# An mLSTM with a bilinear expert layer: a written order for the first two chunks, two more chunks in bfloat16 parts, and weight conversion in written slots beside the first block

## The chip, the core and the metric

The kernel runs on one core of a Trainium2 chip. Its engines are TensorE (PE in the profile; PEld is its weight load), VectorE (DVE), ScalarE (ACT), GpSimd (POOL) and SyncE (SP), which here issues the transfers. The metric is the device time of one execution in microseconds. A change is called faster or slower when it moves the time by more than 2%.

## What is computed

Four sequences of 768 steps with eight heads of 40 columns go through an mLSTM with an exponential input gate and a running maximum; the result, 3072 tokens of 320 columns, goes through a bilinear layer of 1536 columns. The expert weights are float64 in memory, everything else is float32.

```python
for t in range(S):
    m_new = np.maximum(f_gate[:, :, t] + m, i_gate[:, :, t])
    f_stab = np.exp(f_gate[:, :, t] + m - m_new)
    i_stab = np.exp(i_gate[:, :, t] - m_new)
    C = f_stab[..., None, None] * C + i_stab[..., None, None] * np.einsum('bhd,bhe->bhde', vt, kt)
    n = f_stab[..., None] * n + i_stab[..., None] * kt
    h_tilde = np.einsum('bhde,bhe->bhd', C, qt)
    denom = np.maximum(np.abs(nq), 1.0)              # nq = n . q
    y[:, :, t] = sigmoid(o_gate[:, :, t]) * h_tilde / denom
x = y.transpose(0, 2, 1, 3).reshape(B * S, H * D)    # 3072 x 320
out = ((x @ w_a) * (x @ w_b)) @ w_out                # 320 x 1536, 320 x 1536, 1536 x 320
```

## The kernel before

**Chunks.** The time axis is cut into six chunks of 128 steps; with four sequences that makes 24 chunks, numbered n, sequence by sequence within a time chunk. Chunks 0 to 3 are the first time chunk and have no state to read. For each chunk the kernel forms a decay matrix E, the scores q k^T (tile pS), their product with E, the product with the values (pV), the contribution of the carried state (pI, from the second time chunk on), the state's update (pU), the division by the denominator and the output gate (osig), and a transpose (pX) into xh and xl, the two halves that the expert layer reads.

**Two ways for a chunk.** Chunks below NF32 = 6 are computed in float32 (begin_a, begin_b, begin_i, begin_c: float32 transposes pT on TensorE, then float32 matmuls). The others are split into three bfloat16 parts (stage_a, stage_v, stage_b, stage_i, stage_c: the parts are laid out in the tiles qks and turned by DMA transposes into T; products are sums of bfloat16 matmuls). The tiles qks serve two purposes: until the weights are converted they are scratch (step) of the conversion, so stage_a finishes the conversion first. Chunks below NE = 4 get E by one-hot matmuls from stk, which holds the gate sums in three bfloat16 parts (begin_e, tile pE); the others read it from memory (g_dram).

**Blocks.** The expert layer runs in nine blocks of 2, 2, 3, 3, 3, 3, 3, 2 and 3 chunks (moe_block). Each has 12 column groups ff. Per ff there are 16 up matmuls into two PSUM tiles pu (line 693), a copy g (line 699), the product g (line 700), its rounding gh (line 702) and the rest gl (line 704), and two groups later three down matmuls per chunk into pd (line 664). The weights and gh, gl are in the rounded float32 kind.

**Weights.** 32 stages (weight_stages) hold the pieces of w_a, w_b and w_out. A stage is loaded as raw 64-bit words, and turned on the chip into a rounded high part and a low part: ACT reads sign and exponent (line 334), DVE makes the words (lines 335, 336, 338), ACT rounds (line 350), TensorE forms the difference in a PSUM tile pc (lines 352, 353), and DVE adds (line 354). The tiles pu and pc share the pool ps_up of three buffers. For the stages whose rows come from two matrices (last), the parts are put in place by four transfers w<-ct on SP (lines 358, 359).

**What sets the order.** The program is written as generators. The start (function start, 50 steps of priority ahead) is interleaved with the conversion every second piece; afterwards block 0 and 1 are interleaved with pieces of the attention of the following chunks and one piece of conversion in six. The order on each engine is then made by a scheduler that runs a model of the engines and takes what its model has ready, by priority; BEHIND makes the weight loads wait for the issue of certain chunk loads. Each engine executes its own list strictly in order.

The whole gate table is made first (gates): a scan of 768 columns gives the running maximum, and the tables for all chunks follow before the first chunks are multiplied.

## Time and profile before

| | |
|---|---|
| time, median of 3 runs (lowest to highest) | 575.65 us (572.2 to 579.28) |
| the profiled execution, from the first to the last instruction | 572.6 us |
| instructions | 12609 |
| TensorE busy | 547.5 us (96%) |
| VectorE busy | 396.8 us (69%) |
| ScalarE busy | 265.9 us (46%) |
| GpSimd busy | 129.1 us (23%) |
| moved by DMA | 68.34 MB, mean 119 GB/s |
| mean granted TensorE clock | 0.973 |

The page gives the profiled execution's span and no other time for it; the median lies 3.05 us above that span. The busy time of an engine counts the time in which at least one of its instructions runs. A digit of the slices is the busy share of one fortieth of the span, 14.3 us, in tenths. PEclk is the share of the full clock that TensorE was granted. A timeline row has the start and the duration in us, the engine, the line of the kernel, the operation and what it writes and reads; square brackets hold the engine's idle time before it and what ended that. A group row has the busy time in us and the mean duration in ns behind the first bar, and the idle time ahead of the group behind the second. A row of the chain of waits has start and length in us and how many instructions were merged.

### The profile page before, as it was taken

Reading aid. Unit: us, or ns where it says so; the run is one execution under the profiler, and the core shown is the slowest. Engines: PE = TensorE matmul, PEld = TensorE weight load, DVE = VectorE, ACT = ScalarE, POOL = GpSimd, SP = SyncE. Lnnn points to the kernel's source line nnn. Section 1 sums busy time; section 2 is a strip of 40 time slices with the busy share of each in tenths; the row PEclk is TensorE's granted clock in tenths of the full one; section 3 lists DMA queues with packets and bytes.
Section 4 is the critical chain, followed back from the end, with each engine's and each line's share of the span. In section 5 each row is a group of like instructions: output and inputs, shape, how many; then the busy total and the mean of one; then the engine's idle time right before and its main releaser. Section 6 shows DMA issues by size and latency. Waiting matters only on the chain.

```text
span 572.6 us, 12609 instructions
## 1 busy us (share of the span) xinstructions
PE 547.5 (96%) x4864; PEld 526.0 (92%) x4864; DVE 396.8 (69%) x884; ACT 265.9 (46%) x634; POOL 129.1 (23%) x182
## 2 busy tenths in 40 slices
PE   3799999999999999999999999999999999999997
PEld 2688999889999989999999999999999899999996
DVE  6866788975578777499649976698648654954342
ACT  3644565673255465255825554555525921411111
POOL 3021331463213222123303330332111200200000
PEclk9857999989999999999999999999999999999999
DMA  9979945365244966267954676478538603200000
GB/s 206 285 184 278 228 111 107 73 153 121 63 103 115 190 118 142 75 123 148 155 109 110 150 150 131 115 159 159 109 97 129 154 2 99 59 2 23 1 2 34
DMA packets 199863, 68.34 MB, mean 119 GB/s; under 512 B 184476, under 2 KB 193084, under 8 KB 199804
## 3 DMA queue, kind: packets, MB, share of 16 engines
q1 hardware_dynamic: 199804, 67.55, 54.6%
q8 instruction: 38, 0.62, 0.5%
q14 instruction: 21, 0.17, 0.1%
HBM read 41.11 MB, written 5.97 MB: 82 GB/s over the span
## 4 chain that ended last, share of the span: by engine, by line
PE 85%; DVE 4%; ACT 4%; DMA 3%; issue 1%; SPq 1%; POOL 1%; ACTq 0%; DVEq 0%; POOLq 0%
PE pu L693 45%; PE pd L664 21%; PE pV L503 4%; PE pU L527 3%; PE pS L451 3%; PE pV L807 2%; PE pS L764 2%; PE pX L600 2%; PE pI L477 1%; PE pc L352 1%; DMA qk<-in_k_dram 1%; PE pT L751 1%; ACT gbc L396 1%; DMA T<-qks 1%; DMA gbc<-g_dram 1%
## 5 line engine op out<-in xcount | busy, mean ns | idle before, releaser
L693 PE MATMUL pu<-xh,w 128*128 128x384 f32 (+1 forms) x1080 | 278.1, 325 | 2.8 <-ACT g L699 1.9
L693 PE MATMUL pu<-xl,w 128*128 128x384 f32 (+1 forms) x648 | 208.4, 323 | 0.0
L693 PEld LDWEIGHTS pu<-xh,w 128*128 128x128 f32 x1080 | 192.0, 190 | 5.3 <-ACT g L699 2.9
L664 PE MATMUL pd<-w,gh 128*128 128x320 f32 x576 | 127.2, 311 | 0.0
L700 DVE TENSOR_TENSOR g<-pu,g 128x384 f32<-128x384 f32 (+1 forms) x108 | 54.9, 508 | 100.3 <-ACT g L699 51.6
L693 PEld LDWEIGHTS pu<-xl,w 128*128 128x128 f32 x648 | 123.2, 190 | 0.1
L664 PEld LDWEIGHTS pd<-w,gh 128*128 128x128 f32 x576 | 97.2, 189 | 0.3
L664 PE MATMUL pd<-w,gl 128*128 128x320 f32 x288 | 85.8, 312 | 0.0
L699 ACT COPY g<-pu 128x384 f32<-128x384 f32 (+1 forms) x90 | 39.6, 440 | 95.1 <-PE pu L693 88.3
L396 ACT ACTIVATE gbc<-gbc,gtab 128x128 f32<-128x128 f32 x160 | 49.1, 389 | 16.3 <-POOL gbc L389 16.2
L664 PEld LDWEIGHTS pd<-w,gl 128*128 128x128 f32 x288 | 53.1, 189 | 0.1
L704 DVE TENSOR_TENSOR gl<-g,gh 128x384 fp32r<-128x384 f32 (+1 forms) x92 | 50.6, 550 | 2.1
L493 POOL TENSOR_TENSOR vw<-va,gtab 128x336 f32<-128x336 f32 x14 | 10.8, 769 | 161.7 <-PE pU L527 139.0
L702 DVE CAST gh<-g 128x384 fp32r<-128x384 f32 (+1 forms) x108 | 41.2, 382 | 2.4
L389 POOL TENSOR_SCALAR_AFFINE_SELECT gbc<-gbc 128x1024 f32<-128x1024 f32 x20 | 23.9, 1197 | 61.6 <-DMA va<-in_v_dram 33.2
L579 POOL TENSOR_TENSOR osig<-osig,den 128x320 f32<-128x320 f32 x24 | 19.6, 816 | 65.0 <-DVE den L574 45.8
L418 DVE TENSOR_TENSOR r<-qk,qks 128x320 f32<-128x320 f32 x36 | 18.0, 502 | 19.8 <-ACT qks L414 17.0
L414 ACT CAST qks<-qk 128x320 bf16<-128x320 f32 x36 | 16.3, 452 | 31.2 <-DMA T<-qks 27.7
L673 ACT COPY o<-pd 128x320 f32<-128x320 f32 x24 | 8.8, 434 | 42.9 <-PE pd L664 42.9
L424 ACT COPY qks<-qks 128x640 bf16<-128x640 bf16 x36 | 26.0, 726 | 0.4
L460 DVE TENSOR_TENSOR gbc<-gbc,pb 128x512 f32<-128x512 f32 x36 | 24.5, 704 | 2.3 <-ACT pb L458 2.0
L456 DVE TENSOR_TENSOR gbc<-pS,gbc 128x512 f32<-128x512 f32 x36 | 23.6, 679 | 3.3 <-PE pS L451 3.3
(133 smaller groups left out, 878.9 us busy)
## 6 DMA issues: line engine op xcount, KB each, us to landing
gbc<-g_dram SPq DMA_DIRECT2D x20, 512.0 KB
va<-in_v_dram SPq DMA_DIRECT2D x24, 160.0 KB
qk<-in_q_dram SPq DMA_DIRECT2D x24, 160.0 KB
qk<-in_k_dram SPq DMA_DIRECT2D x24, 160.0 KB
osig<-in_o_gate_dram SPq DMA_DIRECT2D x24, 160.0 KB
raw<-in_moe_w_out_dram SPq DMA_DIRECT2D x12, 320.0 KB
out_dram<-o SPq DMA_DIRECT2D x24, 160.0 KB
raw<-in_moe_w_a_dram SPq DMA_DIRECT2D x8, 384.0 KB
```

Source lines behind the costliest of these rows:

```text
L389: nc.gpsimd.affine_select(E, E, pattern=[[0, H], [1, P]], compare_op=ALU.is_ge, fill=-1e30, base=0, channel_multiplier=-1,)
L396: nc.scalar.activation(E[:, h], E[:, h], AF.Exp, bias=beta[:, h:h + 1])
L424: nc.scalar.copy(qks[:, 0, :, lo:lo + 2 * D], qks[:, 1, :, D - lo:3 * D - lo])
L456: nc.vector.tensor_tensor(E, pS, E, op=ALU.mult)
L460: nc.vector.tensor_tensor(E, E, pb[:, 0], op=ALU.subtract)
L503: nc.tensor.matmul(pv[:, h], pb[i][:, h % HH, :], vb[j][:, h], start=(x == 0), stop=(x == len(terms) - 1),)
L664: nc.tensor.matmul(pd[t][:, 0:DM], a[:, cols], w, start=(ff == 0 and first), stop=(ff == NF - 1 and last),)
L693: nc.tensor.matmul(acc[j], a, r, start=(x == 0), stop=(x == len(terms) - 1),)
L699: (nc.vector.tensor_copy if ff in [1, 2] else nc.scalar.copy)(g, acc[0])
L700: nc.vector.tensor_tensor(g, acc[1], g, op=ALU.mult)
L702: nc.vector.tensor_copy(gh, g)
L704: (nc.gpsimd if kb * 12 + ff < 16 else nc.vector).tensor_tensor(gl, g, gh.bitcast(F32), op=ALU.subtract)
```

## The change

- The first two chunks are emitted in one written order (start), and in_order ties each instruction to the one before it on its engine, so that the scheduler cannot move it. The gates of the first time chunk are computed alone (gates_first); the rest of the table (gates_rest) is cut into pieces that are placed beside block 0. The gate loads go out first, one on SP and one on ACT's queue. Filler matmuls on zeros (busy, and dense for chunks 2 and 3) are added on TensorE.
- NF32 goes from 6 to 4: chunks 4 and 5 are computed in bfloat16 parts, as the later ones.
- The weight stages are listed in the order in which block 0 uses them: a down piece of a group ahead of the up pieces of the next. The conversion is split in four steps, signs, words, leading and rests. Stages 0 to 4 are converted in the start, stages 5 to 31 in a written loop in which each stage has a slot beside seven or eight matmuls of block 0. The loop also places the pieces of gates_rest and, from stage 8 on, one piece of the attention of chunks 2 and 3 per stage.
- The stages with rows of two matrices are put in place by copies on ACT and additions on DVE, 64 rows each, instead of transfers.
- In block 0 gh is made by ACT instead of DVE. load_g is issued later within a chunk (at U), and the product with the output gate is done by DVE for chunks 0 and 1.

```diff
-    NF32 = 6
+    NF32 = 4
...
+    def dense(n, bank, count):
+        if NS <= n < NF32:
+            for _ in range(count):
+                nc.tensor.matmul(bank[:, 0:H * DV], zero[:, 0:P], zero, start=True, stop=True)
...
-        nc.vector.tensor_tensor_scan(m, f, i, -1e30, op0=ALU.add, op1=ALU.max)
+        nc.vector.tensor_tensor_scan(m, f[:, 0:P], i[:, 0:P], -1e30, op0=ALU.add, op1=ALU.max)
...
+        yield from ups(0)
+        for g in range(NG):
+            yield from down(3 * g)
+            if g + 1 < NG:
+                yield from ups(g + 1)
+            yield from down(3 * g + 1)
+            yield from down(3 * g + 2)
...
+        with in_order():
+            rest = start()
...
+    with in_order():
+        for x in range(5, len(stages) + 3):
+            if x < len(stages):
+                words(x)
+                if x + 1 < len(stages):
+                    signs(x + 1)
+                leading(x)
+            for _ in range(4 if x >= 12 else 3):
+                next(lead)
+            if 5 <= x - 2 < len(stages):
+                rests(x - 2)
+            for _ in range(4):
+                next(lead)
+            if x < 14 or x % 3 == 0:
+                next(rest, None)
+            if x >= 8:
+                next(att)
...
-            nc.vector.tensor_copy(gh, g)
+            (nc.vector.tensor_copy if kb > 0 else nc.scalar.copy)(gh, g)
```

The written start, with the generators that it drives, in the order of the text (run(x, k) takes k pieces of x, busy(k) issues k fillers, fetch(k) loads the stages up to k):

```python
busy(13); f, i = gates_load()
load_qk(0); load_qk(1); load_v(0); load_v(1); fetch(2); load_o(0, (0, 1)); fetch(5); load_o(0, (2, 3)); fetch(9)
m0, w = gates_first(f, i); rest = gates_rest(f, i, m0)
run(a0, 1); busy(2); run(a0); busy(2); run(b0, 1); busy(2); run(e0); run(rest, 2); run(begin_a(1)); signs(0)
run(b0); words(0); run(e1); gates_w(w); signs(1); leading(0); run(b1); gate_o(0, slice(0, 2)); rests(0); words(1)
run(begin_c(0)); weigh(0); run(begin_c(1)); leading(1); run(stage_f(0)); signs(2); states.append(stage_u(0))
run(states[0], 1); load(NS); fetch(11); weigh(1); run(stage_f(1)); rests(1); words(2); leading(2)
busy(4); run(d0); busy(4); rests(2); signs(3); words(3); leading(3); states.append(stage_u(1)); run(states[1], 1)
load(NS + 1); fetch(len(stages)); busy(4); run(d1); busy(4); signs(4); rests(3); busy(8); words(4)
gate_o(0, slice(2, B)); rests(4)
```

Three places show how rows move. The first is VectorE's list where the gates begin, at the start of the program; g_f and g_i (after: g_xh, g_xl) are the gate inputs, g_m (after: g_first) the working tile, cx_1_103 holds stk. Before:

```order
L194 SCALAR_TENSOR_TENSOR g_m<-g_f,g_i 32x768
L195 MEMSET g_f 32x1
L196 TENSOR_TENSOR g_f<-g_f,g_m 32x127
L201 TENSOR_TENSOR g_m<-g_i,g_m 32x128
L197 TENSOR_TENSOR g_f<-g_f,g_m 32x127
L198 SCALAR_TENSOR_TENSOR g_m<-one,g_f 32x128
L202 TENSOR_TENSOR g_m<-g_m 32x128
L207 TENSOR_SCALAR g_tab<-g_m 32x128
L211 COPY cx_1_103<-g_m 32x256
L213 TENSOR_TENSOR g_m<-g_m 32x256
L335 TENSOR_SCALAR cw<-qks_90 128x384
L211 COPY cx_1_103<-g_m 32x256
```

After, the same place on VectorE:

```order
L231 SCALAR_TENSOR_TENSOR g_first<-g_xh,g_xl 32x128
L232 TENSOR_TENSOR g_xh<-g_xh,g_first 32x127
L233 MEMSET g_xh 32x1
L234 TENSOR_TENSOR g_xh<-g_xh,g_first 32x127
L235 TENSOR_TENSOR g_first<-g_xl,g_first 32x128
L236 SCALAR_TENSOR_TENSOR g_first<-one,g_xh 32x128
L239 TENSOR_TENSOR g_first<-g_first 32x128
L242 COPY cx_1_103<-g_first 32x256
L245 TENSOR_TENSOR g_first<-g_first 32x256
L242 COPY cx_1_103<-g_first 32x256
L245 TENSOR_TENSOR g_first<-g_first 32x256
L242 COPY cx_1_103<-g_first 32x256
```

The scan over 768 columns has become one over 128, and the conversion (cw) has gone from between the rows that fill stk. The scan of the other 640 columns stands behind the last of these rows.

The second place is VectorE's list in the middle of block 0, at its column group ff = 4; cw, qks and cr belong to the conversion of a stage, w to its last step, g, gh to the block, gbc to a chunk's E. Before:

```order
L700 TENSOR_TENSOR g_4_931<-pu_4_1_908,g_4_931 128x256
L335 TENSOR_SCALAR cw<-qks_91 128x384
L354 TENSOR_TENSOR w_934<-pc_936,cw 128x320
L702 CAST gh_4_960<-g_4_931 128x256
L354 TENSOR_TENSOR w_978<-pc_980,cw 128x384
L336 TENSOR_SCALAR qks_91<-cw 128x384
L338 SCALAR_TENSOR_TENSOR cr<-raw_869,qks_91 128x384
L335 TENSOR_SCALAR cw<-qks_90 128x384
L770 TENSOR_TENSOR gbc_611<-pS_1_1160,gbc_611 128x4x128
```

After, at the same column group:

```order
L410 TENSOR_SCALAR cw<-qks_91 128x384
L411 TENSOR_SCALAR qks_91<-cw 128x384
L413 SCALAR_TENSOR_TENSOR cr<-raw_467,qks_91 128x384
L790 TENSOR_TENSOR g_4_899<-pu_4_1_870,g_4_899 128x256
L442 TENSOR_TENSOR w_864<-pc_940,cw 128x384
L863 TENSOR_TENSOR gbc_636<-pS_0_910,gbc_636 128x4x128
L863 TENSOR_TENSOR gbc_636<-pS_1_911,gbc_636 128x4x128
L410 TENSOR_SCALAR cw<-qks_90 128x384
L411 TENSOR_SCALAR qks_90<-cw 128x384
L413 SCALAR_TENSOR_TENSOR cr<-raw_469,qks_90 128x384
```

The three rows of a stage now stand together, one finishing row (w) of an earlier stage follows each three, gh has left the list, and the E of this place belongs to chunk 2 (before: chunk 4).

The third place is TensorE's list where block 1 ends; pu with 128x256 and pd belong to block 1, pu with 128x384 to block 2, pS to the scores of a chunk, pU to a state. Before:

```order
L664 MATMUL pd_0_1515<-w_1385,gh_9_2226 128x320 x2
L664 MATMUL pd_0_1515<-w_1385,gl_9_2228 128x320
L664 MATMUL pd_1_1516<-w_1385,gh_9_2226 128x320 x2
L664 MATMUL pd_1_1516<-w_1385,gl_9_2228 128x320
L693 MATMUL pu_0_0_2319<-xh_1686,w_366 128x384
L693 MATMUL pu_0_0_2319<-xl_1687,w_366 128x384
```

After, at the end of block 1:

```order
L612 MATMUL pU_2261<-vw_2205,qk_84 64x42 x8
L754 MATMUL pd_0_1540<-w_1370,gh_11_2514 128x320 x2
L754 MATMUL pd_1_1541<-w_1370,gh_11_2514 128x320 x2
L754 MATMUL pd_0_1540<-w_1370,gl_11_2516 128x320
L754 MATMUL pd_1_1541<-w_1370,gl_11_2516 128x320
L529 LDWEIGHTS T_1_2194
L529 MATMUL pS_0_2302<-T_0_2177,T_1_2194 128x128
```

Before, block 2 begins while block 1's last two column groups are still to be summed. After, block 1 ends completely, and the scores, the state product and the value product of chunk 7 and the transpose of chunk 6 stand ahead of the first up matmul of block 2.

More of the change, by code (lines that the diff above doesn't have):

```diff
@@ L1 @@
-from contextlib import ExitStack
+from contextlib import ExitStack, contextmanager, nullcontext
 import concourse.bass as bass
@@ new lines, in leading, with rests @@
+    def leading(x):
+        if not turn(2, x):
+            return
+        n, W, r = held[x]
+        w = ws[x] = rpool.tile([P, 2, n], F32R, tag=f"s{x}", name=f"w{x}")
+        h = w[:, 0]
+        if len(stages[x]) > 1:
+            h = cpool.tile([P, WCH], F32R, tag="ct", name="ct", bufs=2)
+        nc.scalar.copy(h, W)
+        held[x] += [w, h]
+    def rests(x):
+        leading(x)
+        if not turn(3, x):
+            return
+        ready[0] = x + 1
+        n, W, r, w, h = held.pop(x)
+        pc = ps_up.tile([P, NTB], F32, tag="pu", name=f"pc{x}")[:, :n]
+        nc.tensor.matmul(pc, eye[0], r, start=True, stop=False)
+        nc.tensor.matmul(pc, eye[1], h, start=False, stop=True)
+        if len(stages[x]) > 1:
+            for j in range(2):
+                rows, other = (slice(64 * i, 64 * i + 64) for i in (j, 1 - j))
+                nc.scalar.copy(w[rows, j], W[rows])
+                nc.vector.tensor_tensor(w[other, j], pc[rows], W[rows], op=ALU.add)
+        else:
+            nc.vector.tensor_tensor(w[:, 1], pc, W, op=ALU.add)
@@ L361, in weights @@
[L361 to L368 removed]
+                words(x)
                 yield x
             if x > 0:
[L371 removed]
+                rests(x - 1)
                 yield x
@@ L831, in room, with busy, run @@
             return spool.tile([P, H * P], F32, tag="x", name=name)
+        states = []
         def start():
-            g = gates()
-            next(g)
+            warm = ps_dn.tile([P, 512], F32, tag="pd1", name="warm")
+            def busy(count):
+                for _ in range(count):
+                    nc.tensor.matmul(
+                        warm[:, 0:H * DV], zero[:, 0:P], zero, start=True, stop=True
+                    )
+            def run(x, count=99):
+                for _ in range(count):
+                    if next(x, "end") == "end":
+                        return
+            busy(13)
+            f, i = gates_load()
@@ new lines, in start @@
+            run(a0, 1)
+            busy(2)
+            run(a0)
+            busy(2)
+            run(b0, 1)
+            busy(2)
+            run(e0)
+            run(rest, 2)
+            run(begin_a(1))
+            signs(0)
+            run(b0)
+            words(0)
+            run(e1)
+            gates_w(w)
+            signs(1)
+            leading(0)
+            run(b1)
+            gate_o(0, slice(0, 2))
+            rests(0)
+            words(1)
+            run(begin_c(0))
+            weigh(0)
@@ new lines, in start @@
+            run(begin_c(1))
+            leading(1)
+            run(stage_f(0))
+            signs(2)
+            states.append(stage_u(0))
+            run(states[0], 1)
+            load(NS)
+            fetch(11)
+            weigh(1)
+            run(stage_f(1))
+            rests(1)
+            words(2)
+            leading(2)
+            d0, d1 = stage_d(0), stage_d(1)
+            warm = ps_dn.tile([P, 512], F32, tag="pd2", name="warm2")
+            busy(4)
+            run(d0)
+            busy(4)
@@ new lines, in start @@
+            rests(2)
+            signs(3)
+            words(3)
+            leading(3)
+            states.append(stage_u(1))
+            run(states[1], 1)
+            load(NS + 1)
+            fetch(len(stages))
+            busy(4)
+            run(d1)
+            busy(4)
+            signs(4)
+            rests(3)
+            busy(8)
+            words(4)
+            gate_o(0, slice(2, B))
+            rests(4)
+            return rest
+        with in_order():
+            rest = start()
@@ L885, in rest @@
             yield from begin_a(NS)
+            for x in states:
+                yield from x
         else:
```

435 lines of the change are left out of this document (221 added, 214 removed).

## The prediction

> **What bounds the kernel now.** I read the page's busy table first, then its 40 slices, then the windows, then single rows.
>
> ```profile
> PE 547.5 (96%) x4864; PEld 526.0 (92%) x4864; DVE 396.8 (69%) x884; ACT 265.9 (46%) x634; POOL 129.1 (23%) x182
> PE   3799999999999999999999999999999999999997
> PEclk9857999989999999999999999999999999999999
> 0.00:168.30 168.30, 150.14 (x1214) 139.99 (x1215) 126.18 (x309) 89.70 (x212) 49.37 (x82) 0.91 0.70 163
> 30.00:50.00 20.00, 18.72 (x115) 16.48 (x114) 13.83 (x35) 8.87 (x24) 5.59 (x8) 0.52 0.89 201
> 113.00:120.00 7.00, 7.00 (x32) 7.00 (x32) 6.01 (x18) 3.71 (x9) 2.92 (x7) 0.53 0.64 161
> 168.30:230.20 61.90, 59.94 (x571) 56.80 (x570) 44.74 (x96) 33.18 (x79) 16.21 (x21) 1.00 0.66 130
> 230.20:292.10 61.90, 61.89 (x599) 59.70 (x598) 47.58 (x98) 32.14 (x76) 16.60 (x21) 1.00 0.68 129
> ```
>
> In a window row stand its length, then busy time of PE, weight load, DVE, ACT and POOL, the granted clock, the DMA share and GB/s. TensorE bounds the kernel: busy 547.5 of 572.6 us. Its digit is 9 almost throughout, and a block of three chunks takes a full 61.9 us of it (the last window). What can be lost is lost early: until 168.3 us PE is idle for 18.2 us, and in two stretches the clock is half. At 0.52 the 18.72 busy us of 30 to 50 would have taken about 9.7, and the 7.00 us of 113 to 120 about 3.7: 12.3 us in all.
>
> Three single rows split the beginning.
>
> ```profile
> 47.51 0.56 PE L693 MATMUL pu<-xh,w 128*128 128x256 f32 x1
> 124.30 0.48 DVE L354 TENSOR_TENSOR w<-pc,cw 128x320 fp32r<-128x320 f32 x1
> 168.29 0.34 PE L693 MATMUL pu<-xh,w 128*128 128x384 f32 x1
> ```
>
> The first is the first up projection of block 0 (chunks 0 and 1), the second the last weight stage to be finished, the third the first instruction of block 2: blocks 0 and 1 are two chunks wide (256 columns), block 2 is the first with 384. Behind 168.29 both kernels have the same blocks to do. So the forecast is one number: **when does block 2 start after the change**. What follows it is 572.6 - 168.3 = 404.3 us and is taken over unchanged; the windows behind it show no idle PE to win.
>
> **The change, part by part.**
>
> *The start.* Before, the whole gate table comes first:
>
> ```profile
> 4.95 1.75 DVE L194 TENSOR_TENSOR_SCAN g_m<-g_f,g_i 32x768 f32<-32x768 f32 x1 [2.28 <-DMA g_i<-in_i_gate_dram]
> 6.94 1.61 DVE L201 TENSOR_TENSOR g_m<-g_i,g_m 32x128 f32<-32x128 f32 x1
> 9.30 0.28 DVE L202 TENSOR_TENSOR g_m<-g_m 32x128 f32<-32x128 f32 x1
> 12.89 0.28 DVE L211 COPY cx<-g_m 32x256 bf16<-32x256 bf16 x1
> 29.59 1.16 PE L764 MATMUL pS<-T 40*128 40x128 f32 x8 [1.42 <-ACT dec L260]
> ```
>
> The one-hot rows (stk) that the decay matrices are built from are complete at 13.2 us (third L211). After, the first scan has 128 columns instead of 768 (about 0.4 us by its share), the subtraction of L201 no longer runs beside one on GpSimd (0.28 as in L202, not 1.61), and no stage conversion stands between. The scan and the dozen short rows behind it, nearly all of the size of L202 and L211, come to 3.9 us. The gate loads landed at 4.95; now each is the first on a queue of its own (SP, ACT), so I put them at 4.2 and stk near 8.2. Walking each engine's written queue from there, with the durations of the same operations before, gives: chunk 0 multiplied at 12.6, chunk 1 at 15.6, their outputs transposed at 21 and 25, stage 4 converted near 29. I allow one microsecond for waits: block 0 starts at **30 us** instead of 47.5. The 43 filler matmuls lie in PE time that is otherwise waiting; if the waits vanish they cost 43 x 0.14 to 0.28 us, 6 to 12 us, on PE but not on DVE, which sets this stretch.
>
> A rule of the Trainium skill can be weighed here. The page "TensorE: Matmul & The Clock Gate", section "What's actually happening", says that the warm-up costs less than 1% of a typical span. The rows show 12.3 us of half clock, 2.1%. By the page at most 5.7 us could come back, and the sum below would lose 6.6 us of its gain.
>
> *The written block 0.* The other twenty-seven stages are converted beside it, in fixed slots. What does DVE need?
>
> ```profile
> L335 DVE TENSOR_SCALAR cw<-qks 128x384 uint32<-128x384 uint32 x20 | 9.4, 468 | 4.4 <-PE pc L352 4.2 <-ACT qks L334 0.2
> L335 DVE TENSOR_SCALAR cw<-qks 128x320 uint32<-128x320 uint32 x12 | 4.5, 372 | 0.5 <-PE pc L352 0.5
> L336 DVE TENSOR_SCALAR qks<-cw 128x384 uint32<-128x384 uint32 x20 | 7.7, 385 | 0.2
> L336 DVE TENSOR_SCALAR qks<-cw 128x320 uint32<-128x320 uint32 x12 | 4.1, 338 | 0.0
> L338 DVE SCALAR_TENSOR_TENSOR cr<-raw,qks 128x384 fp32r<-128x384 uint32 x20 | 12.1, 606 | 0.2
> L338 DVE SCALAR_TENSOR_TENSOR cr<-raw,qks 128x320 fp32r<-128x320 uint32 x12 | 6.0, 500 | 0.1
> L354 DVE TENSOR_TENSOR w<-pc,cw 128x384 fp32r<-128x384 f32 x16 | 8.8, 550 | 0.6 <-PE pc L353 0.6
> L354 DVE TENSOR_TENSOR w<-pc,cw 128x320 fp32r<-128x320 f32 x12 | 5.8, 486 | 3.5 <-PE pc L353 3.5
> L354 DVE TENSOR_TENSOR ct<-pc,cw 128x384 fp32r<-128x384 f32 x4 | 2.2, 552 | 0.0
> L700 DVE TENSOR_TENSOR g<-pu,g 128x256 f32<-128x256 f32 x36 | 15.0, 418 | 20.4 <-PE pu L693 13.5 <-ACT g L699 6.6
> ```
>
> These nine groups come to 60.6 us for 32 stages, 1.9 each: 51 for 27. Eleven g products add 4.6. The rest of the gates, two chunks' float32 attention and two additions on 64 rows each for three stages I put at 14 from the same kinds of row. That is 70 by rows; DVE's rows overlap their neighbours by some 0.08 us, so 63 to 65 on the clock. PE has less:
>
> ```profile
> 125.78 1.92 PE pu L693 x16
> 181.66 1.31 PE pd L664 x9
> 60.09 0.34 PE L352 MATMUL pc<-cr,eye 128*128 128x384 f32 x1
> 60.27 0.34 PE L353 MATMUL pc<-w,eye 128*128 128x384 f32 x1
> L764 PE MATMUL pS<-T,T 40*128 40x128 f32 x64 | 8.4, 288 | 0.0
> L807 PE MATMUL pV<-va,gbc 128*128 128x42 f32 x96 | 14.1, 308 | 0.0
> L451 PE MATMUL pS<-T,T 120*128 120x128 bf16 x288 | 20.3, 220 | 0.0
> L477 PE MATMUL pI<-cx,T 120*128 120x42 bf16 x288 | 10.3, 181 | 0.9 <-DVE gbc L456 0.9
> 189.30 1.22 PE pV L503 x48
> L460 DVE TENSOR_TENSOR gbc<-gbc,pb 128x512 f32<-128x512 f32 x36 | 24.5, 704 | 2.3 <-ACT pb L458 2.0
> L462 DVE TENSOR_TENSOR pb<-gbc 128x512 bf16<-128x512 f32 x36 | 24.8, 689 | 0.0
> L782 PE MATMUL pI<-cst,T 40*128 40x42 f32 x32 | 4.5, 285 | 0.0
> ```
>
> The order has 176 up (0.12 each) and 60 down (0.146) matmuls here, 27 stages at 0.35, and chunks 2 and 3: 21 + 9 + 9.5 + about 12, some 52 us at full clock. So DVE sets this stretch, and the written order lets PE run ahead only as far as the three buffers of ps_up, which the up products and the conversions (pc) share. Behind a DVE that waits stands every later conversion, and PE with it: I take **65 us**, block 0 reaching the end of conversion at 95 instead of 124. Moving gh to ScalarE takes 12 rows off DVE; ACT, busy 89.70 of 168.3 before, has the room. If it had not, DVE would wait about 0.3 us a time, 4 us in all.
>
> *Chunks 4 and 5 in bfloat16.* A chunk's scores, state product and value product cost 8.4/4 + 4.5/2 + 14.1/6, 6.7 us, in float32 (L764's form with two T tiles is that of chunks 2 to 5) and 20.3/18 + 10.3/18 + 1.22, 2.9 us, in parts. PE gains 7.6 us on two chunks and gives 2.5 us back for 18 dense matmuls of 0.14. DVE pays two rows each of L460 and L462 a chunk, 2.8 us, and the residues of the split, about 1 us more. But these chunks were done by 124 before; now they wait until the conversion is over, because their splitting uses the conversion's scratch. Behind 95 us remain 208 up and 84 down matmuls, 25 + 12.3 us, and chunks 4 to 7, 4 x 2.9 plus states and transposes, some 15 to 18: 52 to 56 us of PE, with DVE at 45 beside it. I take **56 us**.
>
> Sum: 30 + 65 + 56 = 151 instead of 168.3, 17.3 us less. The span becomes 555.3. The median of the three runs lies 3.05 us above the profiled span; carried over, **558.4 us**, 3.0% below 575.65. A check from the whole: DVE was busy 126.18 us until block 2, 75% of that time. What is added (splitting) and taken away (gh, copies of T) leaves some 130, of which 23 are done by 30 us; the other 107, at 88% use, end at 152.
>
> The rest counts nothing. Loading the weights is covered by DVE: a stage of 384 KB takes 2.0 us at the 201 GB/s of 30 to 50, less than the 65/27 = 2.4 us that a stage now has; uncovered, a late stage would stop the row it is due in and everything behind. The 16 transfers w<-ct leave SP's queue, and eight copies on 64 rows come to ACT instead, which has the room.
>
> **Rivals.**
>
> (a) *The hand order fits better than I think.* DVE waits for nothing (62) and PE is bound afterwards (52), start 29: 143, so 550. For it: PE is busy 61.89 of 61.9 us in a steady block. Against: three engines near 90% at once.
>
> (b) *The late chunks arrive late.* The gain of the start is given back at the end of block 1.
>
> ```profile
> 119.63 7.21 SPq L428 DMA_TRANSPOSE T<-qks  x4
> 132.47 1.07 PE L451 MATMUL pS<-T,T 120*128 120x128 bf16 x16
> ```
>
> Four transposes take 7.2 us to issue, and the scores follow 12.8 us after the first. Three chunks in series behind 95 + 5 us, each at 12.5 us with 10 for the last one's products, give 148 unhindered; with queues in front, 164. For it: the order puts chunk 7's scores between block 1's end and block 2. Against: steady blocks feed three chunks in 61.9 us. Then 30 + 65 + 69: 571.
>
> (c) *Slower: TensorE stays at half clock through block 0.* In the 65 us stretch PE has 52 us of work, spread with gaps. At half clock this is 104, and PE, not DVE, sets it: 30 + 102 + 56 = 188, so 595. It decides from a mean clock of 52/65 = 0.80 downward; more than 2% slower needs below about 0.57. For it: 30 to 50 stayed at 0.52 although PE was busy 18.72 of 20, and the drop followed an idle time of only 1.42 us (the L764 row). Against: the dense up projections at 47.5 to 51 brought it back.
>
> The same page, section "What's actually happening", has the clock fall only after an idle window of about 3.4 us; by that, (c) could not happen. The 1.42 us row speaks against the page, so (c) keeps its chance.
>
> (d) *It doesn't start earlier:* the first stages land too late. Five stages, the gates, two chunks of q, k and v and the output gates are some 3.8 MB. At the 163 GB/s of the first window that is 23 us, and stage 4 is due at 28; a third less throughput would shift block 0 by 6 to 10 us: 568.
>
> **How the numbers follow.** Forecast 0.55 (551 to 566), (a) 0.20, (b) 0.15, (c) 0.06, (d) 0.04. The range leaves out (c) and the outermost of (a): 546 to 573. A change under 2%, 11.5 us, can hardly be told from none here, as the three runs spread over 7 us. Faster by more (below 564.1): 0.85 of the forecast plus (a), a little of the rest, 0.69. Within: 0.25. Slower: (c), 0.06.
>
> **What would show it.** Right: first 256-column up projection near 30 us, last conversion near 95, first 384-column one near 151; DVE above 0.85 busy in 30 to 95 with PE's idle time released by DVE or ACT; PEclk above 0.8 there; block periods of 61.9 us unchanged. Wrong: PE idle on pX or xh, xl before block 2 (b), a clock near 0.5 in the slices of block 0 (c), or ACT waiting for raw transfers before 30 us (d).

## The result and the profile after

The changed kernel takes **580.26 us** (median of 20 runs, 576.7 to 585.91) against 574.09 us (20 runs, 571.4 to 579.28) for the kernel before on the same chip. The ratio is 1.0091, with a 95% interval of 1.0066 to 1.0116: 0.9% slower, where 3% faster was forecast. That is less than the 2% by which a change is called slower, but the interval leaves out 1.

The profiled execution of the changed kernel, from its page (span, busy table, PE and its clock in 40 slices):

```profile
span 580.5 us, 12898 instructions
PE 546.9 (94%) x4973; PEld 519.7 (90%) x4973; DVE 403.2 (69%) x880; ACT 285.7 (49%) x683; POOL 134.1 (23%) x190
PE   8968798999969989999999999999999999999997
PEclk9788997999988999999999999999999999999999
```

TensorE is busy for as long as before (546.9 us against 547.5), in a span that is 8 us longer. All but two digits below 9 stand in the first twelve slices, 174 us; one is in the fifteenth, one at the end. The three moments that the prediction named stand in the timeline; the windows answer to those shown of before (length, busy time of PE, weight load, DVE, ACT and POOL, clock, DMA share, GB/s):

```profile
30.36 0.28 PE L783 MATMUL pu<-xh,w 128*128 128x256 f32 x1
104.72 0.49 DVE L442 TENSOR_TENSOR w<-pc,cw 128x320 fp32r<-128x320 f32 x1 [1.56 <-PE pc L435]
176.41 1.31 PE L783 MATMUL pu<-xh,w 128*128 128x384 f32 x3
0.00:176.40 176.40, 151.04 (x1370) 134.71 (x1371) 133.69 (x305) 108.42 (x262) 54.45 (x90) 0.91 0.71 159
30.00:50.00 20.00, 14.81 (x109) 13.74 (x110) 18.81 (x41) 13.94 (x30) 2.49 (x4) 0.91 1.03 276
176.40:238.30 61.90, 59.33 (x533) 56.65 (x530) 45.35 (x96) 33.34 (x79) 16.27 (x21) 0.98 0.76 136
238.30:300.20 61.90, 61.17 (x594) 58.89 (x593) 46.88 (x98) 33.84 (x79) 16.34 (x21) 1.00 0.64 133
```

Block 0 starts at 30.4 us as forecast, 17 us earlier than before. The conversion ends at 104.7 instead of the forecast 95, and block 2 starts at 176.4 instead of 151. Behind it 404.1 us follow, 404.3 before. So the start is right, the tail is right, and the middle lost 25 us against the forecast: 9.4 in the stretch to the end of the conversion (74.4 instead of 65), 15.7 behind it (71.7 instead of 56). Until block 2 TensorE was busy for 151.0 us, as long as before (150.1), but of 176.4 us instead of 168.3. The half clock of 30 to 50 is gone (0.91 instead of 0.52); in its place TensorE stands idle for 5.2 of the 20 us.

Two windows and the list of waits of the changed kernel in 30 to 105 us (in a row of waits: total us, times, longest) show what the engines did meanwhile:

```profile
30.00:105.00 75.00, 62.16 (x434) 56.17 (x435) 62.98 (x144) 47.36 (x116) 16.28 (x26) 0.89 0.53 143
105.00:120.00 15.00, 13.80 (x130) 12.62 (x129) 5.01 (x13) 7.87 (x23) 9.76 (x13) 1.00 0.57 113
ACT cb L630 <- DMA c_dram<-cb: 4.2, 1, 4.2
PE pc L434 <- DVE w L442: 6.0, 5, 2.2
PE pc L434 <- ACT g L789: 3.1, 1, 3.1
DVE cw L410 <- ACT qks L401: 3.6, 2, 3.4
DVE w L442 <- PE pc L435: 3.1, 3, 1.6
```

VectorE was busy for 63 us, the work that I had counted, but it needed 75 for it. TensorE stood idle for 13. Each waits for the other, and both for ScalarE: its cast of the state's parts (cb, line 630) waited 4.2 us for a transfer, with the sign steps behind it in its row. That cast belongs to chunk 1's state, which is split only because chunk 5 is now in bfloat16. The prediction had counted no such wait.

From the end of the conversion to block 2 TensorE was busy for 62.5 us, where the prediction had 52 to 56 us of work, and at a mean clock of 0.94:

```profile
104.70:176.40 71.70, 62.49 (x722) 58.42 (x722) 49.79 (x107) 45.46 (x115) 33.85 (x43) 0.94 0.76 158
```

At the start of this stretch, from 105 to 120 us, VectorE has almost nothing to do (5.0 of 15 us), yet chunk 4, on which block 2 depends, doesn't move. Its first rows, from the timelines of ACT, DVE and SP:

```profile
97.06 0.46 ACT L492 CAST qks<-qk 128x320 bf16<-128x320 f32 x1 [1.03 <-DMA qk<-in_q_dram]
109.59 0.17 DVE L653 TENSOR_SCALAR den<-pV 128x8 f32<-128x8 f32 x1 [2.61 <-PE pV L900]
111.03 0.49 DVE L669 TENSOR_TENSOR osig<-pV,osig 128x320 f32<-128x320 f32 x1 [0.84 <-POOL osig L668]
111.44 0.63 DVE L496 TENSOR_TENSOR r<-qk,qks 128x320 f32<-128x320 f32 x1
115.70 1.66 SPq L506 DMA_TRANSPOSE T<-qks  x1
```

The cast of chunk 4's q is done at 97.5. The subtraction that follows it (line 496) runs at 111.4, because ahead of it in VectorE's row stand the denominator and gate of chunk 3, which wait for TensorE and GpSimd. The transposes follow at 115.7, and the three chunks of block 2 come one after another behind them.

### The profile page after: what moved, and what is told of

Read it like the earlier page. It is cut to its first block, busy times and chain, and to the rows that moved or that the text cites. A ratio compares the mean times of both kernels' runs of the same rounds, so it can differ in the third digit from the quotient of the medians.

```text
span 580.5 us, 12898 instructions
## 1 busy us (share of the span) xinstructions
PE 546.9 (94%) x4973; PEld 519.7 (90%) x4973; DVE 403.2 (69%) x880; ACT 285.7 (49%) x683; POOL 134.1 (23%) x190
## 4 chain that ended last, share of the span: by engine, by line
PE 54%; ACT 4%; DMA 3%; SPq 1%; issue 1%; DVE 1%; ACTq 0%
PE pu L783 32%; PE pd L754 15%; PE pV L587 3%; PE pS L529 2%; PE pU L612 1%; ACT gbc L475 1%; DMA qk<-in_k_dram 1%; PE pI L555 1%; PE pX L688 1%; DMA T<-qks 1%; SPq L506 1%; DMA osig<-in_o_gate_dram 1%; SPq L190 0%; ACT qks L502 0%; ACT L475 0%
## 5 line engine op out<-in xcount | busy, mean ns | idle before, releaser
L783 PE MATMUL pu<-xh,w 128*128 128x384 f32 (+1 forms) x1080 | 281.0, 327 | 4.0 <-ACT g L789 2.1
L783 PEld LDWEIGHTS pu<-xh,w 128*128 128x128 f32 x1080 | 194.7, 192 | 7.0 <-ACT g L789 3.1
L754 PE MATMUL pd<-w,gh 128*128 128x320 f32 x576 | 130.0, 312 | 0.0
L783 PEld LDWEIGHTS pu<-xl,w 128*128 128x128 f32 x648 | 124.3, 192 | 1.8 <-DVE xl L693 1.4
L569 POOL TENSOR_TENSOR vw<-va,gtab 128x336 f32<-128x336 f32 x20 | 15.8, 789 | 161.3 <-PE pU L612 145.4
L792 DVE CAST gh<-g 128x384 fp32r<-128x384 f32 (+1 forms) x96 | 37.1, 387 | 2.3
L668 POOL TENSOR_TENSOR osig<-osig,den 128x320 f32<-128x320 f32 x22 | 17.5, 796 | 70.3 <-DVE den L655 50.8
L587 PEld LDWEIGHTS <-pb 128*128 128x128 bf16 x640 | 26.2, 97 | 6.8 <-issue 4.0
L587 PE MATMUL pV<-va,pb 128*128 128x42 bf16 x320 | 28.5, 184 | 3.9 <-DVE num L559 1.7
L538 DVE TENSOR_TENSOR gbc<-gbc,pb 128x512 f32<-128x512 f32 x40 | 27.9, 722 | 4.1 <-ACT pb L536 3.8
L502 ACT COPY qks<-qks 128x640 bf16<-128x640 bf16 x40 | 28.8, 728 | 0.5
```

What stands on the lines that cost most here:

```text
L502: nc.scalar.copy(qks[:, 0, :, lo:lo + 2 * D], qks[:, 1, :, D - lo:3 * D - lo])
L538: nc.vector.tensor_tensor(E, E, pb[:, 0], op=ALU.subtract)
L587: nc.tensor.matmul(pv[:, h], pb[i][:, h % HH, :], vb[j][:, h], start=(x == 0), stop=(x == len(terms) - 1),)
L754: nc.tensor.matmul(pd[t][:, 0:DM], a[:, cols], w, start=(ff == 0 and first), stop=(ff == NF - 1 and last),)
L783: nc.tensor.matmul(acc[j], a, r, start=(x == 0), stop=(x == len(terms) - 1),)
L792: (nc.vector.tensor_copy if kb > 0 else nc.scalar.copy)(gh, g)
```

## The experiments

The table has the moments of each run that are compared below, read from its timelines (first up projection of block 0, last converted stage, first copy of block 0's output, first row of block 2; us), and the measured time with its ratio to the kernel before on the same chip. The runs stand on several chips, on which the kernel before took between 574.1 and 575.6 us; differences of a microsecond or two between rows are read from the ratios, not from the times.

| run | block 0 | conversion | output 0 | block 2 | time | ratio, 95% interval |
|---|---|---|---|---|---|---|
| before | 47.5 | 124.3 | 132.2 | 168.3 | 574.1 | 1 |
| after | 30.4 | 104.7 | 120.0 | 176.4 | 580.3 | 1.0091 (1.0066 to 1.0116) |
| e1 | 30.8 | 106.8 | 114.7 | 169.2 | 574.7 | 0.9985 (0.9952 to 1.0019) |
| e2 | 46.0 | 106.9 | 134.4 | 175.4 | 580.2 | 1.0088 (1.0054 to 1.0123) |
| e3 | 38.1 | 105.4 | 111.9 | 161.8 | 566.9 | 0.9832 (0.9775 to 0.9890) |
| e4 | 42.9 | 118.4 | 127.4 | 165.6 | 570.0 | 0.9898 (0.9837 to 0.9958) |
| e5 | 38.0 | 108.9 | 116.6 | 161.7 | 568.3 | 0.9872 (0.9792 to 0.9952) |
| e6 | 30.5 | 119.8 | 133.7 | 180.4 | 587.0 | 1.0207 (1.0132 to 1.0281) |
| e7 | 32.4 | 105.7 | 112.3 | 162.1 | 566.8 | 0.9847 (0.9776 to 0.9917) |
| e8 | 33.9 | 104.2 | 116.1 | 173.7 | 581.3 | 1.0108 (1.0070 to 1.0146) |
| e9 | 37.7 | 104.1 | 115.8 | 163.0 | 568.2 | 0.9879 (0.9805 to 0.9952) |
| e10 | 41.6 | 119.3 | 123.7 | 163.2 | 569.4 | 0.9887 (0.9821 to 0.9953) |
| e11 | 29.9 | 100.4 | 112.7 | 171.8 | 577.5 | 1.0053 (1.0019 to 1.0086) |
| e12 | 37.5 | 110.6 | 120.0 | 162.0 | 566.6 | 0.9838 (0.9782 to 0.9893) |
| e13 | 37.1 | 107.3 | 117.5 | 166.9 | 579.9 | 1.0107 (1.0041 to 1.0172) |
| e14 | 38.0 | 106.6 | 116.1 | 169.1 | 572.3 | 0.9956 (0.9925 to 0.9986) |
| e15 | 37.5 | 98.9 | 109.1 | 167.0 | 573.3 | 0.9969 (0.9937 to 1.0001) |
| e16 | 39.2 | 109.0 | 116.5 | 161.0 | 567.3 | 0.9865 (0.9811 to 0.9920) |
| e17 | 37.7 | 112.6 | 118.4 | 157.4 | 562.7 | 0.9789 (0.9749 to 0.9828) |
| e18 | 37.6 | 105.6 | 114.0 | 153.8 | 561.2 | 0.9767 (0.9732 to 0.9802) |

### Which part costs: the bfloat16 chunks, the written loop, or the start (e1 to e5)

e1, on the changed kernel (e2 makes the reverse edit on the kernel before):

```diff
-    NF32 = 4
+    NF32 = 6
```

> The changed kernel with chunks 4 and 5 computed in float32 as before (NF32 = 6); start and written block 0 unchanged. Theory 1 (the bfloat16 chunks cost the time): chunk 4 no longer waits for the end of the conversion, the states of chunks 0 and 1 aren't split beside block 0 (ScalarE lost 4.2 us there waiting for a transfer), and block 2 waits for chunk 6 alone. Conversion ends near 100 instead of 104.7, then 58 us of TensorE work plus 5 for float32: block 2 at about 163 instead of 176.4, time 564 to 570. Theory 2 (the written order of block 0 costs it, through waits and a low clock): conversion still ends at 103 to 105, and what float32 adds on TensorE makes up for a shorter chain: 576 to 584.

> The kernel before with only NF32 = 4: chunks 4 and 5 in bfloat16 parts, start and block 0 as before. Theory 1: chunk 4 has to wait for the end of the conversion, which was at 124 us; three chunks at 13 us each after that put block 2 at 180 or later instead of 168.3: 585 to 600. Theory 2: the bfloat16 chunks do no harm, TensorE saves 5 us: 569 to 575.

e3, on the changed kernel:

```diff
-    with in_order():
+    with nullcontext():
         for x in range(5, len(stages) + 3):
```

> The changed kernel, but the loop that writes block 0 with the conversion of stages 5 to 31 is emitted without the ties that hold each engine to the written order; the scheduler may move its instructions. Theory 1: the order is not what costs; block 2 is still bound by the chunks behind the conversion: 574 to 584. Theory 2: the in-order waits go (12.5 us of idle TensorE in 30 to 105): 562 to 571.

e4, with NF32 = 6, the pacing of block 1's chunk pieces (units) as in the kernel before, and the written loop replaced:

```diff
-    with in_order():
-        for x in range(5, len(stages) + 3):
-            ...
+    for x in rest:
+        pass
+    at = 0
+    while at is not None and at < 8:
+        at = next(conv, None)
...
+            if x % 6 == 0:
+                next(conv, None)
```

> The written start alone: chunks 4 and 5 in float32, block 0 interleaved with the conversion as the kernel before does it (one piece each six matmuls, no written order behind the start). If the start's gain of 17 us (block 0 at 30.4 instead of 47.5) is worth what it seems: block 2 at 151 to 156, time 556 to 562. If the start only moves a wait (weight loads or DVE's conversion set the end of block 0 anyway): conversion still ends near 120 and the time is 570 to 576.

e5 is e3 with NF32 = 6.

> Both of the two edits that helped alone: block 0's loop without the written order, and chunks 4 and 5 in float32. If the two losses are separate (13.4 us and 5.5 us against the changed kernel), they add: 580.3 - 13.4 - 5.5 = 561, 558 to 564. If they are one loss seen twice (TensorE has nothing to do until the late chunks come, and either edit fills that hole), it stays at 565 to 569.

**The two chunks in bfloat16** cost 5.5 us in the changed kernel (580.3 against 574.7 in e1) and 5.1 alone (e2 against before). e1 missed its numbers: block 2 came at 169, not 163, and the conversion ended no earlier although ScalarE's wait of 4.2 us is gone with the split of the states. e2 went the expected way, less far: the finished conversion that chunk 4 asks for pulled the conversion forward to 106.9, and the chunks followed from there. NF32 also sets the number of dense fillers (18 with 4, 42 with 6), so the float32 chunks of e1 came with 24 more fillers; the 5.5 us are the balance of both. **The written loop** costs 13.4 us (e3), within the range of the second theory (562 to 571). **The start** brought 5.1 us in e4, not 13 to 19. But e4 is no clean measure of an early block 0: its free loop lets block 0 begin at 42.9, only 4.6 us ahead of before, and its conversion ends at 118. It also keeps the new order of the stages, which no run varied alone.

e3 shows where the written loop loses. Window rows, the last stage, chunk 4's first subtraction and transpose, and block 2's first row of e3:

```profile
30.00:105.00 75.00, 69.87 (x560) 60.67 (x560) 68.90 (x157) 56.20 (x141) 23.12 (x33) 1.00 0.64 171
105.40 0.48 DVE L442 TENSOR_TENSOR w<-pc,cw 128x320 fp32r<-128x320 f32 x1
102.85 0.49 DVE L496 TENSOR_TENSOR r<-qk,qks 128x320 f32<-128x320 f32 x1
105.99 2.70 SPq L506 DMA_TRANSPOSE T<-qks  x2
161.79 0.90 PE L783 MATMUL pu<-xh,w 128*128 128x384 f32 x3
```

The conversion ends no earlier, 105.4 against 104.7. But by then TensorE was busy for 69.9 us instead of 62.2, at full clock instead of 0.89. VectorE was busy for 68.9 us instead of 63.0, which is only in part more work: the same conversion rows took longer (lines 410 and 411 with 384 columns 531 and 561 ns on average, against 354 and 411 in the changed kernel; the cause is open). Chunk 4's first transposes go out at 106.0 instead of 115.7. From the end of the conversion to block 2 it is 56.4 us, the number that the prediction had, instead of 71.7. Block 2 starts just as chunk 6, its last input, arrives, here as in the changed kernel. The stretch and the rows of xl, the second half of a chunk's input to the block, for chunks 4, 5 and 6 of e3:

```profile
105.40:161.80 56.40, 51.07 (x611) 48.40 (x610) 45.44 (x95) 36.08 (x94) 25.48 (x33) 1.00 0.79 160
133.84 0.55 DVE L693 TENSOR_TENSOR xl<-pX,xh 128x384 fp32r<-128x384 f32 x1
147.33 0.55 DVE L693 TENSOR_TENSOR xl<-pX,xh 128x384 fp32r<-128x384 f32 x1
162.09 0.55 DVE L693 TENSOR_TENSOR xl<-pX,xh 128x384 fp32r<-128x384 f32 x1
```

The chunks come 13.5 and 14.8 us apart, no faster than in the changed kernel (13.1 and 13.3, shown further down). Chunk 4 is 15.6 us earlier (133.8 against 149.4), and block 2 follows with 14.6. Chunks 2 and 3, which the written loop hands out piece by piece, have their rows of xl at 74.8 and 91.3 in e3 and at 106.4 and 116.0 in the changed kernel.

With the written loop gone, float32 brings nothing more as long as its fillers come with it. e5 is no faster than e3 (568.3 and 566.9): with both chunks in float32 and 24 more dense fillers, TensorE is the one that is full, from 30 us on almost to block 2 at 161.7.

```profile
30.00:105.00 75.00, 74.64 (x588) 64.00 (x587) 65.35 (x155) 54.33 (x137) 19.02 (x28) 1.00 0.65 168
105.00:120.00 15.00, 15.00 (x124) 14.13 (x123) 5.71 (x13) 7.38 (x15) 3.87 (x5) 1.00 0.34 94
120.00:161.70 41.70, 40.14 (x408) 38.46 (x408) 31.16 (x69) 23.82 (x65) 17.84 (x24) 1.00 0.68 128
```

These are e5's windows: 1.9 us of idle TensorE in 131.7, where e3 has 10.5 in 131.8. So e3 and e5 start block 2 at the same moment for two reasons, the chain of chunks in one and TensorE in the other.

### Is it the pace, the beginning or the fillers (e6 to e8)

```diff
-            if False:
+            if 8 <= x < 20:
                 next(att)
```

> The changed kernel, loop of block 0 in written order, with one number changed: two pieces of the attention of chunks 2 and 3 instead of one in each of the slots 8 to 19. Theory 1 (the written loop hands out chunks 2 and 3 too late, so that block 1 can't start before 116 us although the conversion ends at 105 in every kernel): their inputs xh and xl are ready by 95 instead of 106 and 114, block 0 ends near 112, block 2 starts 5 to 9 us earlier: 571 to 576. Theory 2 (the order itself, an instruction that waits with everything behind it, costs the 13 us): more pieces in the same queues make more waits, the conversion ends later than 105, and the time is 580 or more.

e7 is e3 with each instruction of the loop tied behind the last one of the start on its engine (behind() in place of nullcontext()).

> As the run with the free block 0 (566.9 us), but every instruction of the loop is tied behind the last one of the start on its engine, so that the scheduler can't mix them into the start: first up projection back at 30 instead of 38. If an early block 0 is worth its microseconds: 559 to 564. If the end of the conversion on VectorE (105 in all kernels) decides and not the beginning of block 0: 565 to 570, within 2 us of that run.

e8, on the changed kernel:

```diff
-            for _ in range(count):
+            for _ in range(0):
                 nc.tensor.matmul(bank[:, 0:H * DV], zero[:, 0:P], zero, start=True, stop=True)
...
-                for _ in range(count):
+                for _ in range(min(count, 1)):
                     nc.tensor.matmul(
```

> The changed kernel without its filler matmuls: the dense ones ahead of the scores and products of chunks 2 and 3 are gone, and of each group of warm ones in the start one is left. It computes the same. If they hold up TensorE's clock: the start runs at half clock for longer, block 0 starts 2 to 6 us later and the time is 581 to 587. If the clock doesn't follow them: the same start, and 18 x 0.14 to 0.35 us less behind: 576 to 580.

e6 speaks against the pace: with more of the chunks in the same written rows the conversion ends 15 us later and the time is 587.0. e7 moves block 0 forward by 5.7 us against e3 and gains nothing (566.8): its chunk 4 is no earlier (xl at 134.6, 133.8 in e3), and chunk 6 and block 2 come at 162 in both. e8 starts block 0 3.6 us later and loses nothing that can be measured (581.3 against 580.3), but it also takes 18 dense fillers out of what follows. An earlier block 0 by itself is worth nothing in the free loop (e7); the prediction's first term was right as a moment and wrong as a gain.

### Which engine's written order costs (e9, e13 to e15)

In each of the four, in_order ties only some engines in the loop; e9:

```diff
-    def in_order():
+    def in_order(keep=lambda e: True):
...
+            if not keep(i.engine):
+                continue
             if i.engine in tail:
...
-    with in_order():
+    with in_order(lambda e: e == nc.tensor.engine):
         for x in range(5, len(stages) + 3):
```

> The changed kernel, but in block 0's loop only TensorE's instructions are held to the written order; VectorE, ScalarE, GpSimd and the queues may be reordered. Theory 1 (TensorE's written order costs: it stands at a conversion's two matmuls while a projection of another row could run): as slow as the changed kernel, 576 to 584. Theory 2 (the order of VectorE and ScalarE costs: a copy that waits for a transfer or a subtraction holds up every sign step behind it): as fast as the free loop, 565 to 571.

> The changed kernel with only VectorE held to the written order in block 0's loop. Theory A (VectorE's row is the one that costs: rows of chunk 3 that wait for TensorE's products stand ahead of the last stages and of chunk 4's first subtraction): 575 to 582, chunk 4's first transposes at 110 us or later. Theory B (ScalarE's or SP's row costs): 565 to 571.

> The same with only ScalarE held to the written order. Theory B (ScalarE's row costs: the copy that waited 4.2 us for a transfer of the state, and the leading parts that wait for VectorE, stand ahead of every later sign step): 574 to 582. Theory A: 565 to 571. If both this and the run with VectorE alone stay below 571, it takes several engines' rows together to make the loss.

> The same with only GpSimd and the queue of SyncE held to the written order: 565 to 571 if the loss comes from VectorE or ScalarE; 574 or more if it comes from loads that wait behind others on SyncE's queue (it issued nothing from 94.9 to 109.6 us in the changed kernel).

Against the free loop's 566.9 us, the median rises by 1.3 us with TensorE's order (its interval overlaps that of e3), 5.4 with ScalarE's, 6.4 with that of GpSimd and SyncE, and 13.0 with VectorE's, as much as with all of them together; by the ratios, which allow for the chip, each rise is 1.4 to 2.8 us larger. So theory A's time came. The sign by which it was to be seen did not: in e13 chunk 4's first transpose goes out at 105.7, not after 110, and block 2 begins at 166.9. The output of block 2 is copied at 236.8 us there, at 227.5 in e3 and at 242.9 in the changed kernel, so 9 of the 13 us are lost by then and the rest in later blocks, whose order the scheduler found anew.

In the changed kernel the loss lies ahead of block 2, and there VectorE's order doesn't stand out. Against e3, block 2 is 14.6 us late with all engines tied, 7.3 with ScalarE, 5.2 with GpSimd and SyncE, 5.1 with VectorE and 1.2 with TensorE. Each of these programs has a new order outside the tied rows, so a few microseconds between them mean little. It is shown that VectorE's order alone can cost as much time as all of them, and that no single engine's order makes block 2 as late as all of them do; which rows are out of place is not shown.

### What sets the early part once the loop is free (e10 to e12, e16 to e18)

e10 (on e3) and e11 (on the changed kernel) take the conversion's scratch out of the chunks' tiles; stage_a no longer runs the conversion to its end:

```diff
-        t = step[x % len(step)][:, :n]
         words = raw.bitcast(U32).rearrange("p (n w) -> p n w", w=2)
+        t = words[:, :, 1].bitcast(F32)
```

> The free loop (566.9 us), and the conversion's sign step writes over the high words of the raw weights instead of into the tiles qks of the bfloat16 chunks. So chunk 4's splitting no longer waits for the last stage. If the three chunks in series behind the conversion (first transpose at 106 us, 14 us a chunk, block 2 at 162) set the time: chunk 4 goes ahead beside the conversion, block 2 at 152 to 157, 557 to 562. If TensorE's work behind 105 us is the bound anyway: 564 to 568. If reading every second word costs VectorE time, the conversion ends later than 105 and the time is above 568.

> The changed kernel with its written block 0, and the sign step in place as in the run above. If chunk 4's wait for the conversion is the larger part of the loss: 566 to 572. If the written order keeps chunks 2 to 4 late whatever the scratch is (chunk 4's pieces stand behind the loop): 576 to 582.

e12 is e3 with NF32 = 5.

> The free loop with chunk 4 in float32 and chunks 5 on in bfloat16 (NF32 = 5): between the free loop (three chunks in series behind the conversion, TensorE idle for 5 us of 105 to 162) and the one with both in float32 (TensorE full from 105 to 161.7). Two chunks in series end near 150, TensorE has 2.5 us less work than with two float32 chunks: block 2 at 157 to 160, 562 to 565. If the order the scheduler finds matters more than the bound: 565 to 570.

e16, on e12 (eye[0] holds 2^-52):

```diff
-        nc.vector.scalar_tensor_tensor(r, lo, 2.0 ** -52, t, op0=ALU.mult, op1=ALU.mult)
+        if x >= 5 and x % 2 == 0:
+            nc.scalar.copy(lo.bitcast(F32), lo)
+            nc.gpsimd.tensor_tensor(r, lo.bitcast(F32), t, op=ALU.mult)
+        else:
+            nc.vector.tensor_tensor(r, lo, t, op=ALU.mult)
```

> The free loop with chunk 4 alone in float32 (566.55 us), and for every second stage from the sixth on the product cr moved from VectorE to GpSimd, with a conversion of the low words on ScalarE ahead of it (the factor 2^-52 goes into the matrix eye). VectorE has 7 us less to do before the conversion ends. If VectorE's conversion sets the early part in every version: it ends near 103 instead of 110.5, and 560 to 564. If TensorE's work sets it by now: 565 to 568. If GpSimd's slower rows (0.75 us for 336 elements) put a new wait into each stage: above 569.

e17 is e12, and e18 is e5, both with:

```diff
-        if NS <= n < NF32:
+        if False:
             for _ in range(count):
```

> The free loop with chunk 4 in float32 (566.55 us) without its 30 dense matmuls ahead of scores and products. TensorE was busy 74.6 of 75 us from 30 to 105 there, so if TensorE's work now sets the time, 30 x 0.14 = 4.2 us come off: 561 to 564. If the clock needs them, it falls in that stretch and the time is 567 to 572. If the chunks' chain or VectorE sets the time: 566 to 567.

> The free loop with chunks 4 and 5 in float32 (568.3 us) without its 42 dense matmuls. TensorE was without idle time there from 30 to 120 us; 42 x 0.14 = 5.9 us of it go: 561 to 565 if TensorE's work sets the time, 568 or more if the clock needs the fillers.

e10 fulfils its condition and not its forecast: chunk 4's transposes go out at 91.8, ahead of the end of the conversion, and the conversion, with rows of these chunks between its own, ends only at 119.3; block 2 is no earlier. The time lies in the range that was named for slower conversion rows (above 568), but these are not slower: lines 409 and 410 with 384 columns take 467 and 496 ns up to 125 us, the same two rows of e3 504 and 547. In e11 the written loop keeps chunk 4's transposes at 110.4, and 2.8 us are won (2.2 by the ratios, whose intervals overlap). e12 is within 0.3 us of e3, though its chunk 6 arrives (xl) at 152.2, 9.7 us ahead of block 2; here the chain of chunks is no longer the limit. e16 takes work off VectorE, and the time doesn't follow (567.3 against 566.6). So taking away the wait for the scratch, or work from VectorE, gains nothing in the free versions. e17 and e18 show what does once float32 has shortened the chain of chunks: without 30 and 42 dense matmuls the time falls by 3.8 and 7.2 us (2.8 and 6.0 by the ratios), against 4.2 and 5.9 worked out from their durations. The intervals of the ratios overlap (e12 and e17, e5 and e18), but block 2 moves with the time, by 4.6 and 7.9 us. The windows of e18 and its first row of block 2:

```profile
30.00:105.00 75.00, 74.43 (x605) 66.70 (x605) 66.53 (x162) 58.49 (x143) 20.41 (x30) 1.00 0.74 184
105.00:120.00 15.00, 15.00 (x124) 14.04 (x124) 7.33 (x19) 6.67 (x19) 7.25 (x11) 1.00 0.09 28
120.00:153.80 33.80, 32.74 (x346) 31.71 (x344) 25.41 (x58) 20.11 (x53) 12.98 (x17) 1.00 0.79 146
153.79 0.42 PE L783 MATMUL pu<-xh,w 128*128 128x384 f32 x1
```

TensorE is as full as in e5 (74.4 of 75 us, then 15 of 15, then 32.7 of 33.8), the clock is 1.00 without the fillers, and from 30 us to block 2 TensorE is busy for 7.6 us less, where block 2 is 7.9 us earlier. This is shown for e5 and e18; e17 has 5.1 us of idle TensorE up to block 2, so there it is not TensorE's work alone. At 561.2 us, e18 is the fastest version: 2.3% faster than before (ratio 0.9767, 0.9732 to 0.9802, so 2% is not quite sure). It keeps the written start and the new order of the stages, and takes back the written loop, the bfloat16 chunks and the dense fillers.

## Why the prediction was wrong, step by step

- **The bound.** "When does block 2 start", with the tail taken over, was the right question: behind that moment it is 404.1 us instead of 404.3. In e13 it is 411.2, so this isn't a law.
- **The start, 30 us: right** (30.36), and not by luck: stk was complete at 7.7 us (8.2 in the walk), chunks 0 and 1 multiplied at 12.4 and 15.3 (12.6 and 15.6), their outputs transposed at 21.9 and 26.1 (21 and 25). The last marks are a microsecond late, in a stretch with a mean clock of 0.89, which the walk did not have. As a gain the term was wrong: in e7 5.7 us more of it don't reach the end. The sum took each stretch as a chain whose beginning moves its end. But block 2 waits for chunk 6 (after, e3, e7) or for TensorE's work (e5, e18), and an earlier block 0 moves neither.
- **The written block 0, 65 us: wrong by 9.4.** The work was sized right (63 to 65 us of VectorE, 62.98 in the trace). The failed step is "DVE sets this stretch", that is, VectorE works without waiting. The doubt stood in the prediction ("behind a DVE that waits stands every later conversion") and was priced at nothing. VectorE was at work for 84% of 30 to 105 us, where the sum needed nearly all of it. Yet the free loop too ends its conversion at 105, and no run ends it before 98.9 (e15); what the written order loses is what the other engines do in that time.
- **Chunks 4 to 7, 56 us: wrong by 15.7, the largest miss.** The failed step is that TensorE's work sets this stretch. What sets it is when chunk 4 begins and how long chunks 4, 5 and 6 take one after another. e3 hits the number (56.4), in part by luck: TensorE was busy for 51.1 us of it, a little under the 52 to 56, and the chunks filled the rest. The number holds only if chunks 2 and 3 are through when the conversion ends and chunk 4 can start. In the changed kernel block 0's output is copied at 120.0, 15 us after the conversion, and chunk 4's transposes start at 115.7. I had read from the order that chunk 4's pieces stand behind the conversion, and not from VectorE's row what stands ahead of them. The check from the whole failed in the same way: 107 us of VectorE at 88% use were to end at 152; from 30 us to block 2 it was busy for 112.5 of 146.4 us, 77%.
- **Rival (b) was what happened**, with 0.15: 69 us against 71.7 measured, at the end of block 1 as said. Its reason, three chunks in series of 12.5 us each, is seen in the changed kernel's rows of xl for chunks 4, 5 and 6, 13.2 us apart, the last one 0.65 us ahead of block 2:

```profile
149.40 0.55 DVE L693 TENSOR_TENSOR xl<-pX,xh 128x384 fp32r<-128x384 f32 x1
162.47 0.55 DVE L693 TENSOR_TENSOR xl<-pX,xh 128x384 fp32r<-128x384 f32 x1
175.76 0.55 DVE L693 TENSOR_TENSOR xl<-pX,xh 128x384 fp32r<-128x384 f32 x1
```

To reach 580 it took the 9.4 us of block 0 on top, which no case of mine combined with (b). The sign named for (b), TensorE idle on pX, xh or xl, was hardly there: behind the conversion these waits come to 2.3 us, while TensorE waited 5.6 us inside the chunks, at their value products (pV), for VectorE and ScalarE.
- **The bfloat16 chunks** were put at 5 us less on TensorE and 2.8 to 4 more on VectorE, so nearly even. They cost 5 us in the changed kernel and in the kernel before (e1, e2; e1 with 24 more fillers) and nothing in the free loop with all its fillers (e5 against e3). Without dense fillers block 2 comes earlier with two float32 chunks than with one (153.8 in e18, 157.4 in e17); a free loop with none of either was not run. The state's split for chunks 0 and 1 was not counted.
- **The fillers** were called free as long as TensorE waits. That is right for the changed kernel (e8), and the price named for the other case, 6 to 12 us for all 43, is of the size that e17 and e18 found for the dense ones of the faster versions.
- **Rival (c), half clock through block 0, did not come,** but a part of it did: 0.89 in 30 to 105. (Its sum counts 102 us where 52 us at half clock are 104.) Rivals (a) and (d) did not come: the conversion was later, not earlier, and block 0 was on time.

## What to carry to other kernels

Moving a stretch forward is worth nothing where something else sets the end; before pricing a start, add up the busiest engine's work to there, and follow the last input of what comes next back to where its chain begins. When an order is written by hand, read each engine's row for instructions that wait on another engine and ask what stands ready behind them. Compare runs at the moment in question as well as in the time: VectorE's order alone cost as much time as all, but a third of it at block 2. Once a wait is gone, filler work that was free is paid in full (e18).

## What the runs showed of the hardware

TensorE's clock fell after a short wait and stayed low under full load. Four rows of the changed kernel and the window of the slow stretch (matmuls with 256 columns and a full array take 0.28 us at a granted clock of 1.00):

```profile
91.61 0.28 PE L783 MATMUL pu<-xh,w 128*128 128x256 f32 x1
93.75 0.64 PE L434 MATMUL pc<-cr,eye 128*128 128x320 f32 x1 [1.87 <-DVE w L442]
103.06 0.41 PE L783 MATMUL pu<-xh,w 128*128 128x256 f32 x1
104.11 0.28 PE L783 MATMUL pu<-xl,w 128*128 128x256 f32 x1
93.75:103.90 10.15, 10.15 (x50) 9.16 (x51) 5.46 (x13) 4.25 (x12) 2.66 (x7) 0.52 0.42 57
```

After 1.87 us without work the rows are slow until 103.9, though TensorE has no idle time of its own in these 10 us. The Trainium skill, page "TensorE: Matmul & The Clock Gate", section "What's actually happening", has the clock fall after an idle window of about 3.4 us and rise after a busy one of the same length. The trace agrees with neither length here. About 5 us of work were lost in these 10 us (an estimate from the clock of 0.52): one reason why the same work took longer in the changed kernel. That the wait of 1.87 us brought the clock down is read from the order in time; no run takes this wait away alone. Three dense fillers ran inside the slow stretch, at 95.3, and e18 without the dense ones ran at 1.00 from 30 to 120 us.
